# Zeros before x, two negations and one column copy on VectorE, and a new order of column pairs in a fused 2-D FFT gate kernel

## The chip, the cores and the metric

The kernel runs on one core of a Trainium2 chip. The metric is device time in microseconds (us) of one launch. Three runs of the kernel before gave 127.18 us as median (126.7 to 127.91). A separate, profiled execution of it took 127.11 us; its span from the first to the last recorded instruction is 125.3 us. All places in time below (such as "at 53.6") count from the start of that span.

## The reference

x has 2048 rows (S) of 1024 values (D), bf16. For each of two weight sets A and B the reference takes the real 2-D FFT of x, multiplies it elementwise by complex weights of 2048 x 513, and transforms back. A gate, one number per row of x, mixes the two results:

```
g = sigmoid((x * gate_w).sum(-1, keepdims=True))
X = rfft2(x);   a = irfft2(X * (A_w_r + 1j*A_w_i));   b = irfft2(X * (B_w_r + 1j*B_w_i))
return g * a + (1 - g) * b
```

## The kernel before, in words

All transforms are matrix products on TensorE (PE) with constant matrices. The program is written as one list of operations per engine (`P.add`); each engine works its own list strictly in order, and waits are derived from the keys that an operation reads (`r`), writes (`w`) or adds to (`a`). So an operation that waits holds up everything behind it on its engine, DMA issues included: those are on the lists of SP, POOL and ACT.

**Stage 1** (L337 to L400). x arrives in four blocks c = 0 to 3, each of four row groups. VectorE (DVE) folds each block (`fold`, L345: sums h = 0 and differences h = 1 of mirrored columns) into one of two halves of XF. PE multiplies the folds with a constant M and its negative (L380), 32 matmuls of 256 columns per block, into four PSUM places u = 2h + j of two banks each. The four places of a block are copied out to FT, 128x1024 at a time, by ScalarE (ACT, L389) or by DVE (L387); DVE has one of the four in each block. The next block writes the same place only after this copy. The negatives of M are made by ACT (`negate`, L359), 512 columns per block.

**Stages 2 to 4** (L425 to L491, `step`). 16 column pairs i are handled in turn: 8 pairs p of the transform along S, for two halves hf of the columns. `fold3` (DVE, L431) makes further sums. `stage2(i)` multiplies FT with F2 (PE, L443 and L452) into a pair of banks b0 and ACT copies it out (L458). `stage4(i)` multiplies this with CK (PE, L473), ACT copies it out as X(i) (L477), and `swap(i)` exchanges the partition halves of X(i) by two DMAs into XS(i). `product(i, 0)` multiplies X(i), and `product(i, 1)` XS(i), with the weights of pair p on DVE (L490, 128x2048). Step i runs stage4(i) and swap(i), then stage2(i + 2). The order of the products is written out in ORDER. Before, stage2 uses banks 0 and 1 for i = 0, 2 to 8, 10, 12 and 14, and banks 6 and 7 for 9, 11, 13 and 15. Column 512 is kept apart: `save512` (POOL, L527 and L528) saves it and puts column 256 in its place, and `star_products` (POOL, L532) multiplies it.

The gate's spectrum (`gate_spectrum`, L502) is collected in bank 6 on PE, two of its parts behind each of the steps 0 to 5, and copied out (L652) at the end.

The weights arrive by 44 DMAs on SP's list in six parts W0 to W5 (rows t = 0, 1 to 3, 4 to 7, 8 to 11, 12 and 13, 14 and 15); pair p needs rows 2p and 2p + 1.

**Stage 5** (`group`, L594, copies L602 and L604): 32 groups of 16 matmuls. Groups 0 to 15 need all products of hf = 0, groups 16 to 31 all of hf = 1. Between them lie the gate's sums (`zsum`, L541), the first column (`col0`, L568) and the star column (L507). **Stages 6 and 7** (L725, L750 and after) make the output rows; DVE makes their right-hand sides, `rbgen` (L581), during stage 5.

Of the kernel before, what the change touches and what calls it, by code (L numbers as in the profile page):

```python
# [234 lines left out]
def bass_gated_mix__spectral_gfnet__spectral_gfnet__prompt_kernel(nc, A_x, A_w_r, A_w_i, B_x, B_w_r, B_w_i, gate_w, out):  # L235
# [63 lines left out]
    XPARTS = {0: ((0, 1), (1, 1), (2, 2)), 1: ((0, 2), (2, 2)), 2: ((0, 4),), 3: ((0, 2), (2, 2))}  # L299
    XALL = [("x", c, q0) for c in range(4) for q0, n in XPARTS[c]]  # L300
    P.add("pool", lambda e: e.memset(DUM[:], 0.0), w=["DUM"])
    P.add("pool", lambda e: e.memset(sl(CL, GRo, [(1, 256)]), 0.0), w=["GRz"])
    def mload(eng, c0, n):
# [9 lines left out]
    load("F2", F2, 0, 1536, cst["F2"].ap(), w=["F2"])  # L313
    dma("sp", "GR", sl(CL, GRo, [(1, 128)], np_=8), AP(gate_w.tensor, gate_w.offset, [[128, 8], [1, 128]]), r=["GRz"], a=["GR"])
    load("CK", CK, 0, 1056, cst["CK"].ap(), w=["CK", "GW2"])
# [21 lines left out]
    def fold(c, q0, n, h):  # L337
        t, o = xloc(c)
        o += q0 * 1024
        fo = (c % 2) * 4096 + q0 * 1024  # L340
        for s in range(2):
            g = 1 - 2 * s
            i0 = sl(t, o + 511 * s, [(1024, n), (256 * g, 2), (g, 128)])
            i1 = sl(t, o + (512 if s else 1023), [(1024, n), (-256 * g, 2), (-g, 128)])
            P.add("dve", lambda e, s=s, i0=i0, i1=i1: e.tensor_tensor(  # L345
                out=sl(XF, fo + h * 512 + s * 256, [(1024, n), (384 - 512 * s, 2), (1, 128)]), in0=i0, in1=i1, op=ALU.subtract if h else ALU.add),
                r=[("x", c, q0)], w=[("xf", c % 2, q, h, s) for q in range(q0, q0 + n)])

# [8 lines left out]

    def negate(c):
        P.add("act", lambda e: e.activation(sl(MM, 2048 + c * 512, [(1, 512)]), sl(MM, c * 512, [(1, 512)]), ACT.Copy, scale=-1.0),  # L359
              r=[("M", c)], w=[("NM", c)])  # L360

    cnt = 0

    def stage1(c):
# [4 lines left out]
        for q0, n in parts:  # L369
            for h in range(2):  # L370
                for j in range(2):
# [13 lines left out]
                    dst = sl(FT, h * 8192 + j * 2048 + 4 * c, [(4096, 2), (16, 128), (1, 4)])  # L385
                    if (h == 1 and j == 0 and c < 3) or (c == 3 and h == 0 and j == 1):
                        P.add("dve", lambda e, s=src, d=dst: e.tensor_copy(d, s), r=[bank(2 * u), bank(2 * u + 1)], a=[("F1", h, j)])  # L387
                    else:
                        P.add("act", lambda e, s=src, d=dst: e.activation(d, s, ACT.Copy), r=[bank(2 * u), bank(2 * u + 1)], a=[("F1", h, j)])  # L389
                if h == 0 and c + 2 < 4 and q0 + n == 4:  # L390
                    negate(c + 2)

# [3 lines left out]
    folds(1)  # L396
    for c in range(4):
        stage1(c)
        if c + 2 < 4:
            folds(c + 2)  # L400

# [23 lines left out]
    def fold3(i, css=(0, 1)):  # L425

        n = len(css)
        for s, op in enumerate((ALU.add, ALU.subtract)):
            src = [sl(FT, 12288 * css[0] + j * 2048 + i * 256, [(12288, n), (1, 256)]) for j in range(2)]
            dst = sl(FT, 12288 * css[0] + s * 2048 + (i - 2) * 256, [(12288, n), (1, 256)]) if i > 1 else sl((EO, VD)[i], 512 * css[0] + 256 * s, [(512, n), (1, 256)])  # L430
            P.add("dve", lambda e, dst=dst, src=src, op=op: e.tensor_tensor(out=dst, in0=src[0], in1=src[1], op=op),  # L431
                  r=[("F1", cs, j) for cs in css for j in range(2)] + [("FR", i)], w=[("E", i, cs, s) for cs in css] + [("FR", i - 2)], a=["VD"] * (i == 1))

    def stage2(i, css=(0, 1), ab=(0, 1)):
        hf, p = divmod(i, 8)
        b0 = 4 if i == 1 else 6 if i in (9, 11, 13, 15) else 0
        if 0 in ab:
# [22 lines left out]

    n4 = 0

    def stage4(i):
        nonlocal n4
        b0 = 2 + 2 * (n4 % 2 if i < STEP5 else 0)
        n4 += 1
        parts = [(1, 0, 1), (0, 1, 1)] if i % 8 == 0 else [(0, 0, 2)]
        for pm in range(2):
# [11 lines left out]
    def swap(i):  # L480
        eng = ("pool", "sp")[i // 8]
# [4 lines left out]
    def product(i, sw):  # L486
        hf, p = divmod(i, 8)
        xt, xo, xk = (MM, XSo(i), ("XS", i % NX)) if sw else (XF, Xo(i), ("X", i % NX))
        at = lambda k: sl(WT[k], 4 * p * RWS[k] + 128 * hf, [(32 * RWS[k], 2), (RWS[k] // 2, 8), (1, 128)])
        P.add("dve", lambda e: e.tensor_tensor(out=at(sw), in0=sl(xt, xo, [(0, 2), (128, 8), (1, 128)]), in1=at(1), op=ALU.mult),  # L490
              r=[xk] + [("c256", p // 4)] * hf + [("W", need[t]) for t in (2 * p, 2 * p + 1)], a=[("prod", sw, hf)])  # L491

# [12 lines left out]
    def star_column(b):  # L505
# [5 lines left out]
        for ri in range(2):  # L511
            dma("pool", "xst", sl(XST, 32, [(1, 32)], p0=1 - ri, np_=64, pstep=2), sl(XST, 0, [(1, 32)], p0=ri, np_=64, pstep=2),
                r=["XST"], **({"a": ["XSS"]} if ri else {"w": ["XSS"]}))
# [8 lines left out]

    def save512(k):

        at = lambda l: sl(WA, 16 * k * RW + l, [(32 * RW, 2), (RW, 16)])
        wk = WK[3 * k:3 * k + 3]
        P.add("pool", lambda e: e.tensor_copy(sl(W5, 16 * k, [(32, 2), (1, 16)]), at(512)), r=wk, w=[("W5", k)])  # L527
        P.add("pool", lambda e: e.tensor_copy(at(512), at(256)), r=wk + [("W5", k)], w=[("c256", k)])  # L528

    def star_products():  # L530
        for sw in range(2):
            P.add("pool", lambda e, sw=sw: e.tensor_tensor(out=sl(PST, sw * 64, [(32, 2), (1, 32)]), in0=sl(XST, 32 * sw, [(0, 2), (1, 32)]),  # L532
                                                           in1=sl(W5, 0, [(32, 2), (1, 32)]), op=ALU.mult),
                  r=["XST", "XSS", ("W5", 0), ("W5", 1)], a=["PST"])
# [21 lines left out]
    def col0(u, sw):  # L556
# [10 lines left out]
        for n, (o, tc, rh) in enumerate(seq):  # L567
            P.add("pe", lambda e, o=o, tc=tc, rh=rh, n=n: e.matmul(o, sl(CL, tc, [(1, 128)]), rh, start=(n == 0), stop=(n == 7)),  # L568
                  r=["CL", "PST", ("prod", sw, 0)], w=[bank(bk)])
        P.add("act", lambda e: e.activation(sl(t, 0, [(RWS[sw], 64)]), ps(o0, [(1, 64)]), ACT.Copy),  # L570
# [16 lines left out]
    def group(u, g, eng):  # L587
        hf = g // 16
        for q in range(8):
            l0 = 8 * g + q  # L590
            o = ps(u * 1024 + q * 128, [(1, 128)])
            for ab in range(2):
                deps = [("prod", ab, hf), "CL"] + [("col0", ab)] * (g == 0)
                P.add("pe", lambda e, o=o, l0=l0, ab=ab: e.matmul(  # L594
# [21 lines left out]
    for i in range(2, 8):  # L616
        fold3(i)
# [5 lines left out]
    def step(i):  # L623
        nonlocal last2
        stage4(i)
        swap(i)
        if i == 5:
            save512(0)

        if i + 2 < 16:  # L630
            last2 = stage2(i + 2)
        if i == 8:
            save512(1)
# [3 lines left out]
    ORDER = (((0, 0),), ((1, 0),), ((2, 0),), ((3, 0), (0, 1)), ((1, 1),), ((2, 1), (4, 0)), ((3, 1), (5, 0)), ((4, 1),),  # L637
             ((5, 1),), ((6, 0), (6, 1)), ((8, 0),), ((7, 0), (7, 1), (8, 1)), ((9, 0), (9, 1)), ((10, 0), (10, 1), (11, 0), (11, 1)))

    def products(i):  # L640
        for n, sw in ORDER[i]:
            product(n, sw)

    last2 = None
    for i in range(8):
        step(i)
        for _ in range(2):
            if gt < 16:
                gate_spectrum(gt)
                gt += 1  # L650
        if i == 5:
            P.add("act", lambda e: e.activation(GSB[:], ps(6 * 512, [(1, 32)]), ACT.Copy), r=[bank(6)], w=["GSB"])  # L652
        products(i)
    for i in range(8, STEP5):
        step(i)
        products(i)
        if i == 12:
            row_sums()
# [15 lines left out]
    groups(1)  # L674
    star_column(2 * spare())
    star_products()
    groups(1)
    for i in (12, 14):
        for sw in range(2):
            product(i, sw)  # L680
    step(15)
    slots.insert(3, 1)
    groups(8)
    for i in (13, 15):
        for sw in range(2):
            product(i, sw)
    zsum(spare(), 0)
    groups(2)
    u = spare()
    for sw in range(2):  # L690
        col0(u, sw)
    gate_mask(0)
    for k, name in enumerate(("DI", "DJ")):
        dma("sp", name, sl(FT, DIo + k * 4096, [(2048, 2), (1, 1024)]).bitcast(u16), cst[name].ap().rearrange("p (a b) -> p a b", a=2), w=[name], after=[last2])
    groups(len(todo))
    for n, g in enumerate(range(16, 32)):
# [189 lines left out]
```

## Time and profile before

| what | value |
|---|---|
| median of three runs | 127.18 us |
| profiled execution: own time, span | 127.11 us, 125.3 us |
| PE, DVE, ACT, POOL busy | 112.7, 101.5, 98.8, 44.0 us |
| DMA engines busy, 5 to 44 us | all the time, 345 to 424 GB/s |
| stage 1, first to last matmul | 5.28 to 22.5 us |
| steps, up to the first matmul of stage 5 | to 53.6 us |
| stage 5 to the first matmul of stage 6 | 53.6 to 89.2 us |
| stages 6 and 7 and the last stores | 89.2 to 125.3 us |

Busy time is an average over stages with different limits. The chain of waits, which is followed back from the last instruction, tells which engine was last at each point; the timeline of an engine tells when its instructions start, and in brackets how long it idled before and for what. Copies overlap a little with the next instruction of their engine, so the distance from start to start is shorter than the duration, and it is the distance that sums up.

### The profile page before, as it was taken

How to read it: one execution, taken by the hardware profiler on the slowest of the kernel's cores; microseconds unless marked ns; L12 is line 12 of the kernel's file. 1: busy time of each engine (PE TensorE's matmuls, PEld its weight loads, DVE VectorE, ACT ScalarE, POOL GpSimd, SP SyncE). 2: the span in 40 equal slices, each digit the busy share in tenths (PEclk: the TensorE clock that was granted, in tenths of full speed). 3: DMA queues.
4: the chain of work that ended last, by engine and by line, in shares of the span. 5: the costliest groups of instructions: out<-in, count | busy, mean ns of one | idle time of the engine just before them, and what ended most of it. 6: DMA issues, size and time to landing. Idle time of an engine off the chain costs nothing.

```text
span 125.3 us, 3710 instructions
## 1 busy us (share of the span) xinstructions
PE 112.7 (90%) x1570; PEld 95.6 (76%) x1570; DVE 101.5 (81%) x157; ACT 98.8 (79%) x118; POOL 44.0 (35%) x53
## 2 busy tenths in 40 slices
PE   0399999799999999999999999999799999999950
PEld 0278787595757765579999999999799989898630
DVE  0578999799693999999999969999844778877890
ACT  4228986699999999999999997779589869687610
POOL 1000010006466803103071000000008999999980
PEclk9999999999999999999999999999999999999995
DMA  3999999999999997349993000000000242426265
GB/s 77 316 414 424 404 345 357 347 350 354 361 367 361 358 379 293 140 136 309 332 404 132 5 0 5 0 5 0 0 5 0 84 159 97 167 103 233 91 239 182
DMA packets 17505, 26.12 MB, mean 208 GB/s; under 512 B 2000, under 2 KB 10960, under 8 KB 17360
## 3 DMA queue, kind: packets, MB, share of 16 engines
q1 hardware_dynamic: 16224, 23.25, 53.0%
q0 software_dynamic: 832, 2.11, 4.6%
q10 hardware_dynamic: 432, 0.52, 1.4%
q8 instruction: 12, 0.20, 0.6%
q14 instruction: 5, 0.04, 0.1%
HBM read 17.48 MB, written 4.19 MB: 173 GB/s over the span
## 4 chain that ended last, share of the span: by engine, by line
PE 71%; DVE 8%; ACT 7%; DMA 5%; issue 3%; SPq 2%; DVEq 0%
PE PS L594 25%; PE PS L750 13%; PE PS L725 12%; PE PS L473 9%; DMA WB<-in_A_x_dram 5%; DVE XF L345 5%; PE PS L443 4%; ACT XF L458 3%; PE PS L502 2%; PE PS L452 2%; ACT XF L477 2%; DVE FT L387 2%; SPq L290 2%; PE PS L380 2%; PE PS L541 1%
## 5 line engine op out<-in xcount | busy, mean ns | idle before, releaser
L802 POOL TENSOR_TENSOR WA<-WA 128x512 bf16<-128x512 f32 x22 | 27.3, 1291 | 28.4 <-DVE WA L797 28.2
L594 PE MATMUL PS<-CL,WB 128*128 128x128 bf16 x256 | 32.0, 226 | 0.0
L594 PE MATMUL PS<-CL,WA 128*128 128x128 bf16 x256 | 31.8, 223 | 0.0
L594 PEld LDWEIGHTS PS<-CL,WB 128*128 128x128 bf16 x256 | 31.3, 145 | 0.6 <-issue 0.4
L594 PEld LDWEIGHTS PS<-CL,WA 128*128 128x128 bf16 x256 | 31.4, 145 | 0.1
L604 ACT ACTIVATE WB<-PS 128x1024 bf16<-128x1024 f32 (+1 forms) x29 | 27.9, 1039 | 2.3 <-PE PS L594 2.2
L380 PE MATMUL PS<-MM,XF 128*128 128x256 bf16 x128 | 16.9, 299 | 5.8 <-DVE XF L345 5.3
L490 DVE TENSOR_TENSOR WA<-MM,WA 128x2048 bf16<-128x2048 bf16 x16 | 19.5, 1233 | 2.3 <-DMA MM<-XF 2.3
L735 ACT ACTIVATE WA<-PS 128x1024 bf16<-128x1024 f32 (+1 forms) x16 | 15.8, 997 | 6.7 <-PE PS L725 6.7
L490 DVE TENSOR_TENSOR WB<-XF,WA 128x2048 bf16<-128x2048 bf16 x16 | 19.6, 1233 | 1.0 <-ACT XF L477 1.0
L380 PEld LDWEIGHTS PS<-MM,XF 128*128 128x128 bf16 x128 | 13.4, 107 | 9.0 <-DVE XF L345 5.2
L797 DVE TENSOR_TENSOR WA<-PS,WA 128x512 f32<-128x512 f32 x22 | 14.2, 686 | 6.7 <-ACT WA L757 4.2
L750 PE MATMUL PS<-FT,WA 128*128 128x256 bf16 (+1 forms) x132 | 19.3, 292 | 0.0
L477 ACT ACTIVATE XF<-PS 128x1024 bf16<-128x1024 f32 x16 | 17.4, 1085 | 0.9 <-PE PS L473 0.6
L458 ACT ACTIVATE XF<-PS 128x1024 bf16<-128x1024 f32 x16 | 16.9, 1062 | 0.6 <-PE PS L452 0.6
L473 PE MATMUL PS<-XF,CK 128*128 128x512 bf16 (+1 forms) x72 | 16.5, 356 | 0.6
L750 PEld LDWEIGHTS PS<-FT,WA 128*128 128x128 bf16 x132 | 12.3, 98 | 3.2
L290 POOL DMA_DIRECT2D MM<-XF x16 | 8.9, 555 | 16.3 <-PE PS L473 11.5
L389 ACT ACTIVATE FT<-PS 128x1024 bf16<-128x1024 f32 x12 | 11.6, 1035 | 3.4 <-PE PS L380 3.4
L443 PEld LDWEIGHTS PS<-F,FT 128*128 128x128 bf16 x128 | 7.9, 98 | 4.4 <-ACT XF L458 2.8
L345 DVE TENSOR_TENSOR XF<-WB 128x512 bf16<-128x512 bf16 (+1 forms) x20 | 6.0, 366 | 6.1 <-DMA WB<-in_A_x_dram 6.1
L443 PE MATMUL PS<-F,FT 128*128 128x128 bf16 x128 | 10.0, 220 | 0.1
(74 smaller groups left out, 137.5 us busy)
## 6 DMA issues: line engine op xcount, KB each, us to landing
out_dram<-WA SPq DMA_DIRECT2D x14, 256.0 KB, 2.1
MM<-XF POOLq DMA_DIRECT2D x16, 128.0 KB, 5.4
MM<-XF SPq DMA_DIRECT2D x16, 128.0 KB, 3.5
FT<-c_U SPq DMA_DIRECT2D x1, 2048.0 KB, 10.6
WB<-in_A_x_dram SPq DMA_DIRECT2D x3, 512.0 KB, 6.1
WA<-in_A_w_r_dram SPq DMA_DIRECT2D x4, 256.5 KB, 6.3
WA<-in_A_w_i_dram SPq DMA_DIRECT2D x4, 256.5 KB, 6.5
WA<-in_B_w_r_dram SPq DMA_DIRECT2D x4, 256.5 KB, 6.3
```

Source lines behind the costliest of these rows:

```text
L380: P.add("pe", lambda e, o=o, lh=lh, rh=rh, s=s: e.matmul(o, lh, rh, start=(s == 0), stop=(s == 1)), r=[("xf", c % 2, q, h, s ^ j), ("M", c ...
L443: P.add("pe", lambda e, o=o, cs=cs, j=j, t=t, rh=rh: e.matmul(o, fblock(1 + cs, j, t), rh, start=(j == 0), stop=(j == 1)), r=[("F1", cs, j ...
L458: P.add("act", lambda e: e.activation(dst, src, ACT.Copy), **kw)
L473: P.add("pe", lambda e, o=o, kind=kind, pm=pm, m=m, rh=rh: e.matmul(o, sl(CK, fbo(kind, pm, m), [(1, 128)]), rh, start=(m == 0), stop=(m = ...
L477: P.add("act", lambda e: e.activation(dst, ps(b0 * 512, [(256, 2), (512, 2), (1, 256)]), ACT.Copy), r=[bank(b0), bank(b0 + 1)], w=[("X", i ...
L490: P.add("dve", lambda e: e.tensor_tensor(out=at(sw), in0=sl(xt, xo, [(0, 2), (128, 8), (1, 128)]), in1=at(1), op=ALU.mult), r=[xk] + [("c2 ...
L594: P.add("pe", lambda e, o=o, l0=l0, ab=ab: e.matmul(o, sl(WT[ab], l0, [(RWS[ab] // 2, 128)]), sl(CL, KIo[ab], [(1, 128)]), start=(ab == 0) ...
L604: P.add("act", lambda e, s=src, d=dst: e.activation(d, s, ACT.Copy), r=b, a=["Z"])
L725: P.add("pe", lambda e, o=o, lh=lh, rh=rh, cp=cp: e.matmul(o, lh, rh, start=(cp == 0), stop=(cp == 1)), r=["Z", ("RB", r)], w=[bank(b0 + b ...
L735: P.add("act", lambda e, s=src, d=dst: e.activation(d, s, ACT.Copy), **kw)
L750: P.add("pe", lambda e: e.matmul(ps(col, [(1, n * 256)]), lh, rh, start=(k == 0), stop=(k == last)), r=[("Y", r), "DI"] + ["DJ"] * (full o ...
L802: P.add("pool", lambda e, s=s, op=op: e.tensor_tensor(out=ods(s, 0, 2), in0=pv[:, :, 0, :], in1=pv[:, :, 1, :], op=op), r=[("PQ", pk, 0), ...
```

## The change

Seven edits go together:

- 18 matmuls over zeros (256 columns each, into bank 7) stand at the head of PE's list. They read the part of CL that POOL sets to zero; POOL now does this before the other memset. The load of gate_w into that part now waits for these matmuls.
- `negate` for blocks 2 and 3 becomes one 128x1024 instruction on DVE.
- DVE copies out three places of stage 1, (c, h, j) = (1,0,1), (2,1,1) and (3,0,1), instead of four; block 0 is copied out by ACT alone. The folds of blocks 2 and 3 stand together ahead of blocks 2 and 3 on DVE, and the first four folds of block 2 are 128x512.
- The pairs go in the order SEQ: pair 0 of the second columns (hf = 1) is i = 3, so that pair 7 of the first columns is i = 8 instead of 7. The last products of both halves (i = 8 and 15) are cut in two halves of the columns, and groups wait only for their own half. All of stage2 from i = 2 on uses banks 0 and 1, but for 13 and 15.
- The gate's spectrum has one part per step (two in step 0) and ends in step 10. `fold3(6)` and `fold3(7)` move behind steps 0 and 1, and the keys of fold3 are per j.
- `save512` and `star_products` are on DVE, in steps 1 and 9 and late in the products. The star column's two small DMAs move from POOL to SP.
- The load U5 moves from step 13 to step 15.

```
+    for _ in range(18):
+        P.add("pe", lambda e: e.matmul(ps(7 * 512, [(1, 256)]), sl(CL, GRo, [(1, 128)]), sl(CL, GRo, [(1, 256)]), start=True, stop=True),
+              r=["GRz"], w=[bank(7)])
...
-    dma("sp", "GR", ..., r=["GRz"], a=["GR"])
+    dma("sp", "GR", ..., w=["GRz"], a=["GR"])
...
+        if eng == "dve":
+            P.add("dve", lambda e: e.tensor_scalar(out=dst, in0=src, scalar1=-1.0, scalar2=None, op0=ALU.mult), **kw)
...
-                    if (h == 1 and j == 0 and c < 3) or (c == 3 and h == 0 and j == 1):
+                    if (c, h, j) in ((1, 0, 1), (2, 1, 1), (3, 0, 1)):
...
-    for c in range(4):
-        stage1(c)
-        if c + 2 < 4:
-            folds(c + 2)
+    negate(2, 2, "dve")
+    stage1(0)
+    stage1(1)
+    fold(2, 0, 2, 0)
+    fold(2, 2, 2, 0)
+    fold(2, 0, 4, 1)
+    folds(3)
+    stage1(2)
+    stage1(3)
...
+    SEQ = [(0, 0), (0, 1), (0, 2), (1, 0)] + [(0, p) for p in range(3, 8)] + [(1, p) for p in range(1, 8)]
...
-        b0 = 4 if i == 1 else 6 if i in (9, 11, 13, 15) else 0
+        b0 = 4 if i == 1 else 6 if i in (13, 15) else 0
...
-            dma("pool", "xst", ...
+            dma("sp", "xst", ...
...
+        s0, n = ((0, 4), (4, 28))[k]
+        wk = WK[:2] if k == 0 else WK[1:]
+        if part == 0:
+            P.add("dve", lambda e: e.tensor_copy(sl(W5, s0, [(32, 2), (1, n)]), at(512)), r=wk, w=[("W5", k)])
+        else:
+            P.add("dve", lambda e: e.tensor_copy(at(512), at(256)), r=wk + [("W5", k)], w=[("c256", k)])
...
-                deps = [("prod", ab, hf), "CL"] + [("col0", ab)] * (g == 0)
+                deps = [("prod", ab, hf, g // 8 % 2), "CL"] + [("col0", ab)] * (g == 0)
...
-        if i == 13:
+        if i == 15:
             dma("sp", "U5", ...
...
+    ORDER = (((0, 0),), ((1, 0),), ((2, 0),), ((3, 0),), ((0, 1), (4, 0)), ((1, 1), (2, 1), (5, 0)), ((3, 1), (6, 0)), ((4, 1), (7, 0)),
+             ((5, 1), (8, 0, 0, 1)), ((6, 1), (7, 1)), ((8, 1, 0, 1), (8, 0, 1, 1), (8, 1, 1, 1), (9, 0)), ((9, 1), (10, 0)), ((10, 1), (11, 0)), ((11, 1), (12, 0)))
...
+    for a in ((13, 1), (14, 1), (15, 0, 0, 1), (15, 1, 0, 1), (15, 0, 1, 1), (15, 1, 1, 1)):
+        product(*a)
...
```

More of the change, by code (lines that the diff above doesn't have):

```diff
@@ L356, in folds, with negate @@
             fold(c, q0, n, h)
-    def negate(c):
-        P.add("act", lambda e: e.activation(sl(MM, 2048 + c * 512, [(1, 512)]), sl(MM, c * 512, [(1, 512)]), ACT.Copy, scale=-1.0),
-              r=[("M", c)], w=[("NM", c)])
+    def negate(c, n=1, eng="act"):
+        dst, src = sl(MM, 2048 + c * 512, [(1, n * 512)]), sl(MM, c * 512, [(1, n * 512)])
+        kw = dict(r=[("M", k) for k in range(c, c + n)], w=[("NM", k) for k in range(c, c + n)])
+        if eng == "dve":
+            P.add("dve", lambda e: e.tensor_scalar(out=dst, in0=src, scalar1=-1.0, scalar2=None, op0=ALU.mult), **kw)
+        else:
+            P.add("act", lambda e: e.activation(dst, src, ACT.Copy, scale=-1.0), **kw)
     cnt = 0
@@ L484, in swap, with product @@
                 r=[("X", i % NX)], **({"a": [("XS", i % NX)]} if ri else {"w": [("XS", i % NX)]}), after=last1)
-    def product(i, sw):
-        hf, p = divmod(i, 8)
+    def product(i, sw, h0=0, n=2):
+        hf, p = SEQ[i]
         xt, xo, xk = (MM, XSo(i), ("XS", i % NX)) if sw else (XF, Xo(i), ("X", i % NX))
-        at = lambda k: sl(WT[k], 4 * p * RWS[k] + 128 * hf, [(32 * RWS[k], 2), (RWS[k] // 2, 8), (1, 128)])
-        P.add("dve", lambda e: e.tensor_tensor(out=at(sw), in0=sl(xt, xo, [(0, 2), (128, 8), (1, 128)]), in1=at(1), op=ALU.mult),
-              r=[xk] + [("c256", p // 4)] * hf + [("W", need[t]) for t in (2 * p, 2 * p + 1)], a=[("prod", sw, hf)])
+        at = lambda k: sl(WT[k], 4 * p * RWS[k] + 128 * hf + 64 * h0, [(32 * RWS[k], 2), (RWS[k] // 2, 8), (1, 64 * n)])
+        P.add("dve", lambda e: e.tensor_tensor(out=at(sw), in0=sl(xt, xo + 64 * h0, [(0, 2), (128, 8), (1, 64 * n)]), in1=at(1), op=ALU.mult),
+              r=[xk] + [("c256", p > 0)] * hf + [("W", need[t]) for t in (2 * p, 2 * p + 1)], a=[("prod", sw, hf, h) for h in range(h0, h0 + n)])
     def gate_weights(b):
@@ L521, in row_sums, with save512 @@
         P.add("dve", lambda e: e.tensor_copy(AB[:], AT[:]), r=["AT"], w=["AB"])
[L523 to L528, printed above, removed]
+    def save512(k, part):
+        s0, n = ((0, 4), (4, 28))[k]
+        at = lambda l: sl(WA, s0 * RW + l, [(32 * RW, 2), (RW, n)])
+        wk = WK[:2] if k == 0 else WK[1:]
+        if part == 0:
+            P.add("dve", lambda e: e.tensor_copy(sl(W5, s0, [(32, 2), (1, n)]), at(512)), r=wk, w=[("W5", k)])
+        else:
+            P.add("dve", lambda e: e.tensor_copy(at(512), at(256)), r=wk + [("W5", k)], w=[("c256", k)])
     def star_products():
         for sw in range(2):
-            P.add("pool", lambda e, sw=sw: e.tensor_tensor(out=sl(PST, sw * 64, [(32, 2), (1, 32)]), in0=sl(XST, 32 * sw, [(0, 2), (1, 32)]),
-                                                           in1=sl(W5, 0, [(32, 2), (1, 32)]), op=ALU.mult),
+            P.add("dve", lambda e, sw=sw: e.tensor_tensor(out=sl(PST, sw * 64, [(32, 2), (1, 32)]), in0=sl(XST, 32 * sw, [(0, 2), (1, 32)]),
+                                                          in1=sl(W5, 0, [(32, 2), (1, 32)]), op=ALU.mult),
                   r=["XST", "XSS", ("W5", 0), ("W5", 1)], a=["PST"])
@@ L615, in bass_gated_mix__spectral_gfnet__spectral_gfnet__prompt_kernel @@
                 gate_weights(7)
-    for i in range(2, 8):
+    for i in range(2, 6):
         fold3(i)
@@ L650, in bass_gated_mix__spectral_gfnet__spectral_gfnet__prompt_kernel @@
                 gt += 1
-        if i == 5:
+        if i == 10:
             P.add("act", lambda e: e.activation(GSB[:], ps(6 * 512, [(1, 32)]), ACT.Copy), r=[bank(6)], w=["GSB"])
+        if i in (1, 9):
+            save512(i // 8, 0)
         products(i)
-    for i in range(8, STEP5):
-        step(i)
-        products(i)
+        if i in (1, 9):
+            save512(i // 8, 1)
+        if i < 2:
+            fold3(6 + i)
         if i == 12:
@@ L675, in bass_gated_mix__spectral_gfnet__spectral_gfnet__prompt_kernel @@
     star_column(2 * spare())
+    groups(1)
+    product(12, 1)
+    product(13, 0)
     star_products()
[L677 to L680, printed above, removed]
+    product(14, 0)
     step(15)
@@ L683, in bass_gated_mix__spectral_gfnet__spectral_gfnet__prompt_kernel @@
     groups(8)
-    for i in (13, 15):
-        for sw in range(2):
-            product(i, sw)
+    for a in ((13, 1), (14, 1), (15, 0, 0, 1), (15, 1, 0, 1), (15, 0, 1, 1), (15, 1, 1, 1)):
+        product(*a)
     zsum(spare(), 0)
-    groups(2)
+    gate_mask(0)
+    for k, name in enumerate(("DI", "DJ")):
+        dma("sp", name, sl(FT, DIo + k * 4096, [(2048, 2), (1, 1024)]).bitcast(u16), cst[name].ap().rearrange("p (a b) -> p a b", a=2), w=[name], after=[last2])
+    groups(3)
     u = spare()
@@ L691, in bass_gated_mix__spectral_gfnet__spectral_gfnet__prompt_kernel @@
         col0(u, sw)
[L692 to L695, printed above, removed]
+    groups(3)
     for n, g in enumerate(range(16, 32)):
```

39 lines of the change are left out of this document (14 added, 25 removed).

## The prediction

> **What bounds the kernel now.** I read the chain of waits first, then the timelines of the engines that it names. The chain, columns start and length in us:
>
> ```profile
> 16.72 2.85 DVE XF L345 x8
> 19.58 1.14 DVE FT L387
> 20.72 0.05 issue
> 20.77 1.92 PE PS L380 x16
> ...
> 53.63 1.13 PE PS L594 x16
> ...
> 56.74 7.78 PE PS L594 x128
> ```
>
> DVE sets the time up to 20.7; from 53.6 PE has no gap worth naming before 88.5. So everything turns on when PE gets into stage 5, and on whether something holds it there. DVE's timeline in stage 1:
>
> ```profile
> 12.04 1.22 DVE L387 CAST FT<-PS 128x1024 bf16<-128x1024 f32 x1
> 13.17 2.50 DVE L345 TENSOR_TENSOR XF<-WA 128x1024 bf16<-128x1024 bf16 x4
> 15.59 1.22 DVE L387 CAST FT<-PS 128x1024 bf16<-128x1024 f32 x1
> 16.72 2.85 DVE L345 TENSOR_TENSOR XF<-WA 128x512 bf16<-128x512 bf16 x8
> 19.50 2.34 DVE L387 CAST FT<-PS 128x1024 bf16<-128x1024 f32 x2
> ```
>
> No brackets: DVE idles nowhere from 10.02 (x arrives) on. Start to start, a copy costs 1.14, a 128x1024 fold 0.60, a 128x512 fold 0.34. TensorE's clock in stage 1, from the matmuls of L380 in three equal stretches (two shown; after the stretch come its length, PE's busy time and its matmuls):
>
> ```profile
> 7.60:10.00 2.40, 2.40 (x13) 1.71 (x12) 1.00 1.06 431
> 10.20:12.60 2.40, 2.40 (x24) 2.15 (x23) 1.00 0.98 408
> ```
>
> Matmuls start 213 ns apart until 10.1 and 109 ns apart after it, though the clock column says 1.00 in both. But PE was not the bound there: DVE was.
>
> The steps, ACT's timeline:
>
> ```profile
> 32.23 1.02 ACT L458 ACTIVATE XF<-PS 128x1024 bf16<-128x1024 f32 x1
> ...
> 34.24 1.02 ACT L458 ACTIVATE XF<-PS 128x1024 bf16<-128x1024 f32 x1
> ```
> ```profile
> 51.38 1.17 ACT L458 ACTIVATE XF<-PS 128x1024 bf16<-128x1024 f32 x1
> ...
> 53.18 1.19 ACT L458 ACTIVATE XF<-PS 128x1024 bf16<-128x1024 f32 x1
> ```
> ```profile
> 33.30 0.45 PEld L443 LDWEIGHTS PS<-F,FT 128*128 128x128 bf16 x8 [0.51 <-ACT XF L458]
> ```
>
> Late steps take 1.81, two copies of 0.904: ACT bounds. While stage2 has one bank pair, its weight load waits for the copy (1.02 + 0.05), and the next copy starts 0.94 after: a loop of 2.01 per step, however idle ACT is. Last, what the products wait for:
>
> ```profile
> 48.89 0.49 POOL L527 COPY W<-WA 128x32 bf16<-128x32 bf16 x1 [5.04 <-DMA WA<-in_B_w_i_dram]
> ```
> ```profile
> 70.64 1.22 DVE L490 TENSOR_TENSOR WA<-MM,WA 128x2048 bf16<-128x2048 bf16 x1
> ```
>
> The last weights (W5) are there at 48.9. The last product ends at 71.86, and group 16 starts at 71.9: PE and DVE arrive together.
>
> **Stage 1.** DVE's copy of block 0 goes. In its place comes the negation; a TENSOR_SCALAR of 128x1024 (L550) runs 0.48 and holds the next instruction for 0.40 to 0.51. No row shows it without its per-partition scalar: bounds 0.34 (a 128x512 fold) and 0.60 (a 128x1024 fold), taken 0.40. So 12.04 + 0.40 = 12.44; copy (1,0,1) to 13.58; four folds to 14.92; two to 16.12; eight (2.78) to 18.90; copy (2,1,1) to 20.04. PE: x lets block 1's first half start its second rows at 10.8, so with a fast clock it is through at 12.2, ahead of 12.44. Block 2 has its first half folded at 15.0, with 4 of its matmuls done. From there 60 matmuls remain for PE, 60 x 0.109 = 6.55, to 21.6; the folds (16.2 and 18.95) come before PE needs them (16.4 and 19.8), the banks too: ACT's 10 copies of 0.92 are at most one behind, and (2,1,1) ends 0.7 before its place is needed at 20.7. Before, the last matmul started its 109 ns at 22.4 (20.77 + 16 x 0.109 = 22.52 for the end of issue). Gain **0.92**, and what follows, ACT's last copy, moves with PE.
>
> The zeros run from 1.1 (memset 0.31 after 0.74): 18 x 0.213 = 3.84, to 4.95, under the wait for x (5.28), so they cost nothing; each one more would cost 0.21. SP reaches gate_w's load at 6.50, after them; if they were late, all weights behind it on SP would be. Their use is small: they take the slow matmuls out of block 0, which only (1,0,1) would feel. [...]
>
> **Steps.** Let a be the start of the copy L458 of i = 2: 28.08 before, 27.16 after. Before, the steps to the copy of i = 8 took 12.44 (2.01 and 2.14 in turn: 16 gate matmuls, 0.38 on PE, and L652, 0.30 on ACT), the seven to i = 15 12.66. After, PE has one gate part less in each (-0.19), so the loop of 2.01 binds, and, as 9 and 11 now use banks 0 and 1 too, up to i = 12: 10 x 2.01 = 20.1. Then bank 6, free after L652 (+0.20): copies of 13, 14, 15 at a + 22.2, 24.0, 25.8; stage4(13)'s copy runs from a + 24.93 to a + 25.95 and frees the banks of the first group: a + 26.0 = 53.16, against 53.60 before. So the steps **lose 0.48** of the 0.92. The first 6 steps gain 0.4, the next 4 lose 4 x 0.2, the rest is L652 and the banks. Pair (1,0) at i = 3 takes 8 narrow matmuls for 4 (1.04 against 0.89), inside ACT's slack in the loop.
>
> **From 53 on.** PE's work is the same and has no gap, so 0.44 is kept if DVE has the products. (8,0,0,1) needs W5, so DVE stands still from some 46 to 48.9; the bytes ahead of W5 are the same. Behind it before group 16: 14 full products (1.144: 16.0), six halves (as 128x1024, 0.60: 3.6), row sums 1.53, two copies of save512 and two star products. These small ones have no row on DVE; 0.09 (L521, start to start) to 0.49 (POOL's longer L527) each, taken 0.13, nearest L521: 0.5. Together 21.7: 48.9 + 21.7 = 70.6, 0.8 before PE's 71.44. (8,1,0,1) is done at 52.6, before group 1; (8,0,1,1) at 53.3, and X(14) writes its buffer at 53.9. Then DVE's second halves end at 71.8, as before, and its idle of 1.4 up to 88 takes up the 0.44.
>
> Nothing for: U5 (SP issues it behind swap 15, about 58.5; 10.6 to land makes 69.1, rbgen starts at 72.9); DI and DJ behind it (needed at 91); the star DMAs (swap 15 behind them waits until 57.7 anyway); fold3 (two later pairs, DVE idle there). save512 off POOL lets swap 6 go earlier; nobody waits then.
>
> **Sum.** 127.11 - 0.92 + 0.48 = 126.67. The profiled run is 0.07 under the median, so about **126.7**. Bounds of the negation (-0.06, +0.2; faster than 0.25 it would wait for PE) and of the small ones (four at 0.49: +1.4, of which 0.8 is slack) give 126.5 to 127.3.
>
> **Rivals.**
> - A: zeros do not raise the clock. For it: only real data is in the trace. Then block 1's first half is done at 13.1, as before, copy (1,0,1) waits 0.66, and 126.67 + 0.66 = 127.3. 0.08. [...]
> - B: the bank loop opens, and steps go at ACT's 1.81. Then (8,1,0,1) stops PE at 52.65 instead: gain 0.95, 126.2. Against it: all six waits of L443 name L458. 0.11.
> - C: B, and W5 lands 0.6 sooner, as POOL's swaps move out of its way: groups start at 52.05, group 16 at 70.3; gain 1.55, 125.6. For it: the DMA engines are full until 48. 0.16.
> - D, slower: the weights become the bound. DVE stands in order at (8,0,0,1), with all later products, swaps 12 to 15 (which need buffers that these free) and group 1 behind it; slack 0.8, so from a landing at 49.7 it holds group 16, from 50.2 the kernel is slower than before. With the longest landing in the page (10.7 after issue) on the last issue at 41.55, W5 comes at 52.25, group 16 at 73.95: 2.05 late, 129.2. For it: DVE reaches W5 with one product fewer behind it than before and loses 3 us there. 0.12.
> - Forecast: 0.53.
>
> Range: all but D, 125.5 to 127.7. Faster by over 1% (about what a measurement can tell here; below 125.9) is C: 0.16; slower (above 128.45) is D: 0.12; within, 0.72.
>
> **What would show it.** Right: DVE copies (1,0,1) at 12.4; last L380 near 21.6; L458 every 2.01 from i = 2 to 12; DVE idle for W5 up to 48.9; first L594 near 53.2. Wrong: L380 still 213 ns after 8; L458 at 1.81 before i = 12; a PE gap at group 16; W5 far from 48.9.

## The result, and the profile after

The changed kernel takes 126.15 us as median of 12 runs (125.62 to 126.41); the kernel before, run beside it on the same chip, 127.07. The ratio is 0.992, with a 95% interval of 0.990 to 0.995: 0.9 us faster by the medians, forecast 0.44. (Some runs, of the kernel before above all, were disturbed and took 129 to 135; they are left out of all ratios and medians here, and of the one experiment whose profile fell into such a run only the stretch behind the last matmul is read.)

The profiled execution took 126.23 us, its span 124.3. The chain that ended last, columns start and length:

```profile
13.54 0.98 DVE XF L348 x3
15.02 6.62 PE PS L387 x59
21.72 1.03 ACT FT L396
...
53.17 1.13 PE PS L606 x16
54.37 1.03 PE PS L606 x16
...
88.62 1.96 PE PS L735 x32
```

From 15.0 on PE, not DVE, carries stage 1 (its matmuls are L387 now; L606 is stage 5, L735 stage 6). DVE's timeline there:

```profile
12.07 0.42 DVE L365 TENSOR_SCALAR MM<-MM 128x1024 bf16<-128x1024 bf16 x1
12.41 1.22 DVE L394 CAST FT<-PS 128x1024 bf16<-128x1024 f32 x1
13.54 5.30 DVE L348 TENSOR_TENSOR XF<-WA 128x512 bf16<-128x512 bf16 x14
18.77 2.38 DVE L394 CAST FT<-PS 128x1024 bf16<-128x1024 f32 x2
```

The negation, start to start, is 0.34, and no bracket stands behind the copy at 12.41: PE had its input ready. The zeros on PE's timeline, and then the matmuls L387 from 7.2 to 9.0 (after the stretch its length, and PE's busy time with its matmuls):

```profile
1.10 4.02 PE L304 MATMUL PS<-CL 128*128 128x256 bf16 x18 [1.10 <-POOL DUM L302]
```
```profile
7.20:9.00 1.80, 1.80 (x18) 1.43 (x16) 1.00 1.02 402
```

The kernel before has 10 matmuls in the same stretch. Single records show the pitch, the distance from one matmul's start to the next, falling from 213 to 109 ns at some 7.1; before, at some 10.1. The steps, from ACT's timeline (L470 is the former L458):

```profile
27.03 1.02 ACT L470 ACTIVATE XF<-PS 128x1024 bf16<-128x1024 f32 x1
...
45.11 1.02 ACT L470 ACTIVATE XF<-PS 128x1024 bf16<-128x1024 f32 x1
...
47.12 1.02 ACT L470 ACTIVATE XF<-PS 128x1024 bf16<-128x1024 f32 x1
...
52.85 1.06 ACT L470 ACTIVATE XF<-PS 128x1024 bf16<-128x1024 f32 x1
```

The first line is i = 2, the third i = 12, the last i = 15. Ten steps from i = 2 to i = 12 take 20.09, the loop of 2.01 each. And DVE at the last weights:

```profile
48.89 0.70 DVE L499 TENSOR_TENSOR WB<-XF,WA 128x1024 bf16<-128x1024 bf16 x1 [1.20 <-DMA WA<-in_B_w_i_dram]
49.51 0.20 DVE L538 COPY W<-WA 128x56 bf16<-128x56 bf16 x1
```

W5 is there at 48.89, to the hundredth as before (by chance, as later profiles show). Where the time went, term by term (us, profile against profile):

| stretch | forecast | before | after | measured |
|---|---|---|---|---|
| start of the last stage-1 matmul | -0.92 | 22.41 | 21.36 | -1.05 |
| from there to the first matmul of stage 5 | +0.48 | 31.19 | 31.77 | +0.58 |
| from there to the first of stage 6 | 0 | 35.57 | 35.49 | -0.08 |
| from there to the end of the span | 0 | 36.15 | 35.65 | -0.50 |
| execution outside the span | 0 | 1.79 | 1.96 | +0.17 |
| sum | -0.44 | | | -0.88 |

The steps of the forecast hold within 0.13. The term that it doesn't have is the fourth: within it, the stretch from the last matmul's end to the last packet of the stores took 3.75 before and 3.28 after.

### The profile page after: what moved, and what is told of

Same layout as the page of the kernel before. It is cut to its first block, busy times and chain, and to the rows that moved or that the text cites. A ratio compares the mean times of both kernels' runs of the same rounds, so it can differ in the third digit from the quotient of the medians.

```text
span 124.3 us, 3754 instructions
## 1 busy us (share of the span) xinstructions
PE 116.1 (93%) x1588; PEld 96.6 (78%) x1588; DVE 100.9 (81%) x169; ACT 100.0 (80%) x117; POOL 38.6 (31%) x45
## 4 chain that ended last, share of the span: by engine, by line
PE 73%; ACT 11%; DMA 6%; DVE 4%; issue 2%; SPq 2%; DVEq 0%
PE PS L606 25%; PE PS L760 13%; PE PS L735 12%; ACT XF L470 8%; PE PS L387 7%; PE PS L455 6%; DMA WB<-in_A_x_dram 6%; PE PS L481 4%; PE PS L464 3%; DVE XF L348 2%; SPq L290 2%; DVE WA L771 1%; PE PS L553 1%; ACT FT L396 1%; ACT XF L485 1%
## 5 line engine op out<-in xcount | busy, mean ns | idle before, releaser
L606 PE MATMUL PS<-CL,WB 128*128 128x128 bf16 x256 | 31.9, 226 | 0.0
L606 PE MATMUL PS<-CL,WA 128*128 128x128 bf16 x256 | 31.7, 223 | 0.0
L606 PEld LDWEIGHTS PS<-CL,WB 128*128 128x128 bf16 x256 | 31.3, 145 | 0.6 <-DVE WA L499 0.4
L606 PEld LDWEIGHTS PS<-CL,WA 128*128 128x128 bf16 x256 | 31.4, 145 | 0.1
L499 DVE TENSOR_TENSOR WB<-XF,WA 128x2048 bf16<-128x2048 bf16 (+1 forms) x18 | 20.0, 1110 | 3.6 <-DMA WA<-in_B_w_i_dram 2.1
L499 DVE TENSOR_TENSOR WA<-MM,WA 128x2048 bf16<-128x2048 bf16 (+1 forms) x18 | 19.8, 1111 | 0.6 <-DMA MM<-XF 0.6
L470 ACT ACTIVATE XF<-PS 128x1024 bf16<-128x1024 f32 x16 | 16.3, 1025 | 0.7 <-PE PS L464 0.6
L485 ACT ACTIVATE XF<-PS 128x1024 bf16<-128x1024 f32 x16 | 16.5, 1034 | 0.3 <-PE PS L481 0.2
L387 PE MATMUL PS<-MM,XF 128*128 128x256 bf16 x128 | 16.2, 284 | 0.5 <-DVE XF L348 0.3
L387 PEld LDWEIGHTS PS<-MM,XF 128*128 128x128 bf16 x128 | 12.6, 101 | 4.2 <-DVE XF L348 2.2
L396 ACT ACTIVATE FT<-PS 128x1024 bf16<-128x1024 f32 x13 | 12.4, 1028 | 2.2 <-PE PS L387 2.2
```

The costliest lines, as they stand in the source:

```text
L387: P.add("pe", lambda e, o=o, lh=lh, rh=rh, s=s: e.matmul(o, lh, rh, start=(s == 0), stop=(s == 1)), r=[("xf", c % 2, q, h, s ^ j), ("M", c ...
L470: P.add("act", lambda e: e.activation(dst, src, ACT.Copy), **kw)
L485: P.add("act", lambda e: e.activation(dst, ps(b0 * 512, [(256, 2), (512, 2), (1, 256)]), ACT.Copy), r=[bank(b0), bank(b0 + 1)], w=[("X", i ...
L606: P.add("pe", lambda e, o=o, l0=l0, ab=ab: e.matmul(o, sl(WT[ab], l0, [(RWS[ab] // 2, 128)]), sl(CL, KIo[ab], [(1, 128)]), start=(ab == 0) ...
```

## The experiments

### Stage 1 alone, and all but stage 1

The kernel before with the edits of stage 1 (zeros, negation, order, copies) and nothing else; and the changed kernel with the old stage 1.

```
 b_stage1: before.py, and
+    for _ in range(18): ... matmul over zeros
+    negate(2, 2, "dve")
+    stage1(0); stage1(1); folds of 2 and 3; stage1(2); stage1(3)
+    if (c, h, j) in ((1, 0, 1), (2, 1, 1), (3, 0, 1)):
 a_old_st1: after.py, and these lines as in before.py
```

> The kernel before with the stage 1 of the change alone (zeros, negation on DVE, three copies, order of the folds); pairs, banks, gate, products and column 512 as before. Theory 1: stage 1 ends 1.05 us earlier and the old steps take it along without the 0.5 that the new banks cost, PE would enter stage 5 near 52.6 and group 16 near 70.9; DVE gains too, as its old wait for the swap of pair 2 (2.06 us up to 39.96) gets shorter and W5 lands at 48.9: 0.9 to 1.0 us faster than before. Theory 2: DVE has no slack at group 16 in the old order, it stays bound by DMA landings, and most of the gain is lost there: 0 to 0.4 us faster than before, with a gap of PE ahead of group 16.

> The changed kernel with stage 1 as before: no zeros, both negations of blocks 2 and 3 on ScalarE, the old evictions and the old order. It has the later parts alone: the pair (1,0) at the fourth step, the banks, column 512 and the star products on VectorE, the swaps and halves. Theory 1 (the later parts by themselves lose what the steps lost, 0.58, less the 0.08 of group 16): last stage-1 matmul near 22.4, L470 of i = 2 near 28.1, first matmul of stage 5 near 54.1, stage 6 near 89.7, and if the end behind the last matmul is the 3.3 of the changed kernel, 127.2 in the median; with 3.7, 127.6. Theory 2 (the later parts bring a gain of their own, which stage 1 hides): under 126.9.

Stage 1 alone: 126.28 us, ratio 0.992 (0.987 to 0.996). All but stage 1: 127.06 us, ratio 1.0015 (0.9998 to 1.003). So the whole gain is stage 1's, and the later parts, all together, bring nothing that can be measured: what they lose in the steps they win back at the end, as the profiles below show. The length of stage 1, from DVE's first fold of the last of x to PE's last matmul, settles its term:

| kernel | first fold | last matmul | length |
|---|---|---|---|
| before | 10.02 | 22.41 | 12.39 |
| all but stage 1 | 9.88 | 22.20 | 12.32 |
| stage 1 alone | 10.03 | 21.34 | 11.31 |
| after | 10.05 | 21.36 | 11.31 |

The five other experiments that keep the whole changed stage 1 have 11.31 too; x lands there between 9.69 and 10.06 and moves all of it along. Behind it, all but stage 1 came to stage 5 at 53.97, 31.77 after its last stage-1 matmul, exactly as the changed kernel: the lost half microsecond of the steps is theirs. Its stretch behind the last matmul is 3.30, stage 1 alone has 3.40: both less than the 3.75 of before. That left the cause of the fourth term open, see the last group.

Stage 1 alone did what its first theory says, as far as its profile goes: stage 5 starts at 52.53, group 16 at 70.78, and stage 6 at 88.02, 0.60 before that of the changed kernel. Its profiled run, 125.57, is the faster by 0.66. But its runs spread from 125.27 to 127.10, those of the changed kernel from 125.62 to 126.41, and the medians differ by 0.13 the other way. Its last product ends at 70.76, right at group 16, where the changed kernel has 0.7 to spare (its products of the first halves end at 70.63, group 16 starts at 71.36). That this missing slack makes the spread is likely, but not shown.

### The zeros

```
 a_no_zeros: after.py without            b_zeros: before.py with (and the memsets and gate_w's load as in after.py)
-    for _ in range(18):
-        P.add("pe", lambda e: e.matmul(ps(7 * 512, [(1, 256)]), ... r=["GRz"], w=[bank(7)])
```

> The changed kernel without the 18 matmuls over zeros (gate_w's load then waits for nothing of PE), all else as changed. My theory (rival A of the prediction, turned round): the clock then rises near 10 us as before, block 1's first half is through PE at about 13.0 instead of 12.3, DVE's copy (1,0,1) starts near 13.1 instead of 12.4, and all later stages slide by this: 0.6 to 0.7 us slower than the changed kernel, about 126.8. Rival: PE's clock in stage 1 is hidden anyway, and the time is that of the changed kernel, 126.15.

> The kernel before with the 18 matmuls over zeros alone. Theory 1 (the clock rises near 7 instead of 10, but VectorE bounds stage 1, so nothing follows): last stage-1 matmul 22.3 to 22.4, stage 6 within 0.1 of 89.17, 127.1 to 127.4, ratio 0.998 to 1.002. Theory 2 (the zeros alone carry the gain): last stage-1 matmul before 22.0 and a ratio under 0.996. On the stretch from the last matmul to the last packet of the stores: 3.7 if it belongs to the kernel before's later parts, 3.3 to 3.4 if it goes with the zeros (the run of the stage-1 edits alone had 3.40).

Without zeros the changed kernel takes 126.44 us (ratio 0.994, 0.991 to 0.997); with them the kernel before takes 126.91 (1.0007, 0.997 to 1.004). Without zeros, the same stretch (its matmuls are L384), and then DVE's timeline:

```profile
7.20:9.00 1.80, 1.80 (x11) 1.20 (x9) 1.00 1.00 388
```
```profile
12.17 0.42 DVE L362 TENSOR_SCALAR MM<-MM 128x1024 bf16<-128x1024 bf16 x1
12.69 1.23 DVE L391 CAST FT<-PS 128x1024 bf16<-128x1024 f32 x1
```

PE is slow up to some 9.7 (11 matmuls in that stretch for 18), and DVE's copy starts 0.52 behind the negation instead of 0.34. Stage 1 takes 11.50, so in this profile the zeros are worth 0.19, not the 0.66 of rival A: that figure came from PE's place in the kernel before, and in this run PE was through with that half of block 1 0.4 sooner (its pitch fell 0.4 sooner, too). From the first zero matmul at 1.1 to the fall of the pitch are 2.8 to 6.0 us in the eight traces with zeros. In the kernel before the zeros are worth nothing: with them its pitch had fallen by 5.41 (the first matmuls of stage 1 are 109 ns apart), stage 1 still took 12.40, since DVE bounds it (it idles nowhere from 9.75 to its last copy). Its profile (127.79 us) shows instead a wait that can make times of the kernel before spread. The waits between 64 and 73, columns total, times and longest in us:

```profile
DVE WA L493 <- DMA MM<-XF: 0.8, 1, 0.8
```

and between 64 and 73 in the trace of the kernel before:

```profile
DVE WA L490 <- DMA MM<-XF: 0.2, 1, 0.2
```

The product of the swapped pair 14 waits for its swap, which SP issues behind the 2 MB of U5. As that kernel has no slack at group 16, the 0.8 went on to PE, which waited 0.9 there, and stage 6 came at 90.00 instead of within 0.1 of 89.17.

### The steps: banks and gate parts as before

```
 a_banks: after.py with
-        b0 = 4 if i == 1 else 6 if i in (13, 15) else 0
+        b0 = 4 if i == 1 else 6 if i in (9, 11, 13, 15) else 0
-        for _ in range(2 if i == 0 else 1):
+        for _ in range(2):
-        if i == 10:
+        if i == 5:
```

> The changed kernel with the old banks of stage2 (6 and 7 for i = 9, 11, 13, 15) and the old pace of the gate's spectrum (two parts per step, copied out in step 5). My theory says that the new banks cost 0.5 us: L458's successors at 1.81 from i = 9 on instead of 2.01, first matmul of stage 5 no longer held by banks but by product (8,1,0,1) at 52.73: 0.4 us faster than the changed kernel, about 125.75. Rival: the changed kernel is bound by DVE behind the last weights or by PE elsewhere, and nothing is gained (126.15).

125.72 us in four runs, ratio 0.9875 (0.981 to 0.994), an interval that takes in most of the changed kernel's; profile against profile 0.23 less. The copies of i = 8 to 15 are 1.8 apart again and the first matmul of stage 5 starts at 52.56 for 53.13. Not all of it stays, as the chain shows:

```profile
43.26 5.66 DMA WA<-in_B_w_i_dram
...
49.84 2.29 DVE WA L499 x2
52.13 0.20 DVE WA L540
52.33 0.54 DVE WA L499
52.87 0.05 issue
52.91 1.13 PE PS L606 x15
```

PE's second matmul waits to 52.91: group 1 now hangs on W5 and DVE's queue behind it. Stage 6 starts 0.24 before that of the changed kernel. So the chosen banks, with the gate parts that go with them, do cost 0.6 at the start of stage 5, and 0.35 of it is covered by the weights.

### What the weights and the halves carry

```
 a_late_w5: after.py with the 384 KB load of CL ahead of W5 instead of behind
 a_whole:   after.py with
-    (8, 0, 0, 1) ... (8, 1, 0, 1), (8, 0, 1, 1), (8, 1, 1, 1) ... (15, 0, 0, 1), ... (15, 1, 1, 1)
+    (8, 0) ... (8, 1) ... (15, 0), (15, 1)
```

> The changed kernel with the 384 KB load of CL ahead of the last weights W5 on SP's list instead of behind them: W5 lands about 1.1 us later (384 KB at 357 GB/s), near 50.0. Rival D of the prediction puts the slack at 0.8 at group 16, and 0.4 at group 1 (product (8,1,0,1) ends at 52.73, group 1 starts at 53.13): the kernel gets 0.6 to 0.8 us slower, first at group 1. If the weights are hidden, it is the same (126.15); if the kernel is bound by them now, the whole 1.1 is lost.

> The changed kernel with products 8 and 15 in one piece each, so that groups wait for all of them. By my sum of DVE's work behind W5 (48.9): product (8,1) ends at 53.7, so group 1 starts 0.55 later than 53.13, and the last product ends at 71.8, about when PE arrives at group 16. 0.5 to 0.6 us slower than the changed kernel, about 126.7. Rival: the halves only matter when the banks are not what holds group 1; then it is the same, 126.15.

With the load ahead: 126.51 us, ratio 0.9955 (0.992 to 0.999), its interval overlapping that of the changed kernel; the profiled runs are the same (126.21 and 126.23). W5 in this run, and in the one without zeros:

```profile
49.25 0.70 DVE L501 TENSOR_TENSOR WB<-XF,WA 128x1024 bf16<-128x1024 bf16 x1 [2.72 <-DMA WA<-in_B_w_i_dram]
```
```profile
48.32 0.70 DVE L496 TENSOR_TENSOR WB<-XF,WA 128x1024 bf16<-128x1024 bf16 x1 [1.68 <-DMA WA<-in_B_w_i_dram]
```

W5 came 0.36 later than in the changed kernel, not 1.1. Even that can't be put down to the edit: in the undisturbed profiles in which W5 keeps its place on SP's list it landed anywhere from 47.84 (zeros alone) over 48.32 (no zeros) and 48.89 (before, and after) to 49.36 (all but stage 1). What the run does show is the slack: with W5 at 49.25 the second matmul of stage 5 started at 53.14, right behind the product's end at 53.09. How the kernel does with weights later than that wasn't reached.

Whole products: 127.05 us, ratio 0.997 (0.994 to 1.000). PE at the start of stage 5:

```profile
52.93 0.25 PE L606 MATMUL PS<-CL,WB 128*128 128x128 bf16 x1
54.00 0.27 PE L606 MATMUL PS<-CL,WA 128*128 128x128 bf16 x1 [0.82 <-DVE WA L499]
```

PE stands 0.82 for the second half of the uncut (8,1), which ends at 53.95. Stage 6 starts at 89.45, 0.83 later than in the changed kernel: what is lost at group 1 is not won back. So in the changed kernel the halves are worth 0.8 to 0.9; without them it would hardly have been faster than the one before. What they mend came with the change, though: stage 1 alone, with whole products and the old order of pairs, has no such wait at the start of stage 5.

### A version that takes both

Old banks, the load of the row-sum constants behind all weights, and another order of the products around W5.

```
 a_best and a_best2: after.py with the edits of a_banks, and
-        if t0 == 8:
-            load("CV", ...)          (now behind the last weights)
-    ((5, 1), (8, 0, 0, 1)), ((6, 1), (7, 1)), ((8, 1, 0, 1), (8, 0, 1, 1), ...
 a_best:
+    ((5, 1), (8, 0, 0, 1)), ((8, 1, 0, 1), (6, 1)), ((8, 0, 1, 1), (7, 1), ...
 a_best2:
+    ((5, 1), (6, 1), (8, 0, 0, 1)), ((7, 1),), ((8, 1, 0, 1), (8, 0, 1, 1), ...
```

> The kernel of the run on banks (old banks of stage2, old pace of the gate) with two more edits: the 147 KB load CV goes behind all weights on SP's list, and product (8,1) of the first half is second behind W5, ahead of (6,1); then (8,0) of the second half, then (7,1). W5 should land up to 0.4 earlier, (8,1,0,1) ends 1.4 behind it, near 50.1, instead of 3.8, so group 1 is held by banks again, at 52.5, and X(14)'s buffer is free in time. 0.5 to 0.7 us faster than the changed kernel, 125.5; if DVE's last product stays where it is and PE waits at group 16, no faster than the run on banks (125.72).

The first was a miss: 127.16 us, ratio 0.998 (0.994 to 1.002). W5 landed 0.4 sooner, which lies within the spread above, but DVE could use none of it:

```profile
48.50 0.70 DVE L498 TENSOR_TENSOR WB<-XF,WA 128x1024 bf16<-128x1024 bf16 x1 [1.46 <-DMA WA<-in_B_w_i_dram]
49.12 0.20 DVE L537 COPY W<-WA 128x56 bf16<-128x56 bf16 x1
50.40 1.85 DVE L498 TENSOR_TENSOR WA<-MM,WA 128x1024 bf16<-128x1024 bf16 x2 [1.08 <-DMA MM<-XF]
```
```profile
54.18 0.27 PE L605 MATMUL PS<-CL,WA 128*128 128x128 bf16 x1 [1.74 <-DVE WA L498]
```

DVE waited 1.08 for the swap of pair 8, to which (8,1,0,1) had been moved up, and group 1 also reads (7,1), which had been moved behind (8,0,1,1): an error of the order, not of the banks.

> The changed kernel with the banks of the kernel before (bank 6 for 9, 11, 13, 15; two gate parts a step), the load of the row-sum constants behind all weights, and the product (6,1) put ahead of the wait for W5. Group 1 needs all products of the first eight pairs and their swapped ones, (6,1) and (7,1) too; the run before this one had put (7,1) behind (8,0,1,1), which held group 1 by 1.74. Now (6,1) lies in VectorE's idle time before W5, and behind W5, expected at 48.5, come (8,0,0,1), (7,1), (8,1,0,1), done by 51.3 if the swap of pair 8 is there at 50.4. Theory (group 1 is then held by banks and ScalarE's copies alone): first matmul of group 1 at 52.0 to 52.6 and no wait of its second, stage 6 0.5 to 0.6 before the changed kernel, 125.5 in the median, ratio to the kernel before 0.985. Rival (group 16 takes it back, as VectorE's later products end at 71.4 as before): stage 6 at most 0.25 earlier, 125.9.

125.59 us in five runs (125.38 to 125.62), ratio 0.990 (0.988 to 0.992); profile against profile 0.63 under the changed kernel. DVE around W5, and PE:

```profile
46.07 2.37 DVE L498 TENSOR_TENSOR WA<-MM,WA 128x2048 bf16<-128x2048 bf16 x2
48.58 0.70 DVE L498 TENSOR_TENSOR WB<-XF,WA 128x1024 bf16<-128x1024 bf16 x1
```
```profile
52.47 0.25 PE L605 MATMUL PS<-CL,WB 128*128 128x128 bf16 x1
52.55 0.22 PE L605 MATMUL PS<-CL,WA 128*128 128x128 bf16 x1
```

(6,1) fills what was idle time, no bracket is left, and (8,1,0,1) is done at 51.28, 1.2 before PE comes. Stage 6 starts at 87.98, 0.64 before that of the changed kernel, and the last product ends at 70.41, 0.3 before group 16: the rival, that group 16 takes it back, falls. This is the fastest of all kernels here by its median, though its interval touches that of the changed kernel. Up to stage 6 it only undoes what the later parts had lost: stage 1 alone is there at 88.02. What it has more is slack at group 16, 0.3 where stage 1 alone has 0.02, and its five runs lie within 0.24.

### Behind the last matmul

Two runs asked first whether the 0.47 there is chance, and whether U5 has to do with it: the kernel before once more, unchanged, and with `if i == 15:` for `if i == 13:` at the load U5.

> The kernel before itself, for a second profile of it. The change gained 0.9 us by the runs but 0.44 by my sum; between the two profiles 0.43 us lie behind the last matmul, in one late packet of the last store of before. Theory 1: that packet was chance, and what usually costs the kernel before the other 0.4 us is DVE without slack at group 16: in another profile the tail behind the last matmul is 3.3 as in all other profiles, and PE waits 0.2 to 0.6 us for a product ahead of group 16 (it waited 0.09). Theory 2: the late packet is a trait of before: the tail is 3.7 again. Ratio to before 1.000 within 0.3%.

> The kernel before with the 2 MB load U5 at step 15 instead of 13, nothing else. If the kernel before is held at group 16 by landings on a DVE without slack, the swaps of pairs 12 to 15 land sooner without U5 in their way, DVE's last product ends up to 0.25 us earlier than 71.86, and the time falls by 0 to 0.3 us, with a smaller spread. If PE alone sets the time there, it is the same (127.06).

Unchanged: ratio 1.001 (0.997 to 1.005), stretch 3.71. With U5 late: 126.95 us, ratio 0.998 (0.996 to 1.001), stretch 3.72. So it is no chance, and U5 is not the cause. (Late U5 does take the wait for the swaps away: the last product ended at 71.40 though x landed 0.38 later in that run. In time this can't be told from nothing.)

In the DMA view of the last 7 us, the kernel before has a transfer that the changed one lacks:

```profile
q1 hardware_dynamic: 798, 1.08, 42.8%
q10 hardware_dynamic: 288, 0.39, 15.8%
q14 instruction: 1, 0.01, 0.6%
...
out_dram<-WA SPq DMA_DIRECT2D x3, 256.0 KB, 2.9
...
out_dram<-WA SPq DMA_DIRECT2D x1, 128.0 KB, 2.4
```

It is the line of q14, a fetch of instructions, 8 KB in 0.66, and the stores of SP land 0.5 to 0.7 later than in the changed kernel (2.2 and 1.9). When that fetch starts, against the end of the last matmul, and how many records DVE has in the trace:

| kernel | DVE records | fetch starts | last packet |
|---|---|---|---|
| before; again; zeros alone; U5 late | 198 | -0.58; -0.55; -0.56; -0.58 | 3.75; 3.71; 3.66; 3.72 |
| stage 1 alone | 199 | -0.77 | 3.40 |
| whole products | 207 | -3.14 | 3.33 |
| all but stage 1 | 210 | -4.47 | 3.30 |
| after; five more with its DVE work | 211 | -5.57; -5.53 to -5.55 | 3.28; 3.29 to 3.30 |

The more records DVE has, the sooner the fetch starts: -0.55 to -0.58 with 198, -5.53 to -5.57 with 211. If DVE's instructions are the cause, it needs nothing but more of them:

```
 b_pad: before.py with
+    PAD = sb("PAD", 2, f32)
+    for _ in range(13):
+        P.add("dve", lambda e: e.memset(PAD[:], 0.0), w=["PAD"])
```

> The kernel before with 13 tiny memsets on VectorE at its start, in the 10 us in which it waits for x; nothing else. In the traces so far the stretch from the last matmul to the last packet of the stores is 3.66 to 3.75 where an 8 KB fetch of instructions starts 0.55 to 0.58 before the last matmul's end, 3.40 where it starts 0.77 before it, and 3.28 to 3.32 where it starts 3 or more before it; and the fetch comes the earlier, the more instructions VectorE has (198, 199, 207, 210, 211 records: 0.58, 0.77, 3.14, 4.47, 5.57 before the end). Theory (it is VectorE's code, and fetched that late it takes its place among the last stores): with 211 records the fetch moves to some 5.5 before the end, the stretch becomes 3.3, and the kernel gets 0.4 faster by instructions that do nothing: ratio near 0.997. Rival (the fetch is a bystander, and the stretch goes with other parts): the fetch moves, the stretch stays at 3.7, ratio 1.000; or the fetch doesn't move, and is another engine's.

The fetch moved to -5.37 and the stretch became 3.29, within a hundredth that of the changed kernel. (Another 8 KB fetch starts 4.2 before the last matmul's end in the kernel before and in this one, so that one is not the cause.) The same window of its DMA view has no q14 any more, and

```profile
q1 hardware_dynamic: 772, 1.02, 40.7%
q10 hardware_dynamic: 288, 0.39, 16.0%
...
out_dram<-WA SPq DMA_DIRECT2D x3, 256.0 KB, 2.3
...
out_dram<-WA SPq DMA_DIRECT2D x1, 128.0 KB, 1.9
```

126.70 us against 127.13, ratio 0.998 (0.995 to 1.001): by the medians the size expected, 0.4, though the interval still holds no change. In the profiles it is shown that the stretch depends on where this fetch falls. How 8 KB come to cost 0.47 is only argued: the DMA share is 0.95 from 121 to 124, with the stores, and the last five packets of 2 KB in the kernel before end 0.08 apart, up to 0.37 after all others, as if one DMA engine were behind by the 0.66 that the fetch took.

## Why the prediction was right, and where it was not

The verdict (within 1%) and the range held. The forecast of 126.7 was 0.5 too slow, and the faster rival C (125.6) would have missed by as much; but C's mechanism is not what happened. Stage 1 and the steps went as forecast; that the verdict held as well owes something to luck, since a term left out of the sum is as large as the whole forecast gain.

- **Stage 1**, forecast -0.92, measured -1.05. The bound passed from DVE to PE at 15.0 as put. The negation took 0.34, at the lower bound of its range, not 0.40, but PE still started at 15.02 for 15.0. The 0.13 is one matmul fewer from there on (59 in the chain, not 60: 0.11) and a sum rounded from 21.55 up to 21.6.
- **Steps**, forecast +0.48, measured +0.58. The loop of 2.01 up to i = 12 came out to the hundredth, the three copies behind it within 0.02 when counted from the measured copy of i = 2, 27.03 (49.22, 51.04, 52.85 for 49.23, 51.03, 52.83). ACT's last copy for group 1 ended as put, at 52.99 (27.03 + 26.0 = 53.03), but PE was at the matmuls of stage 4 until 53.13. Rival B, the open loop, falls; with the old banks the copies do run at 1.81.
- **Products.** "So 0.44 is kept if DVE has the products" held; (8,1,0,1) was done at 52.73 for 52.6, the products for group 16 at 70.63 for 70.6. But the slack was put in the wrong place: 0.8 at group 16, while the kernel hangs on group 1, where it was 0.4 (whole products cost 0.8 to 0.9, and W5 0.36 later used all of it). Rival D starts there, from a landing near 49.3, not from 49.7, and so within the spread of landings seen here.
- **W5** at 48.89: rival C's sooner landing did not come in this profile. The hit to the hundredth is luck, as other profiles with W5 in the same place have 47.8 to 49.4.
- **Zeros.** With them the pitch fell to 109 ns at 3.9 to 7.1, without them at 8.7 to 10.1, and rival A falls; but its price, 0.66, was 0.19 in the one profile that tests it. No run had shown by then that zeros bring the pitch down, so the "fast clock" that the sum gives block 1's first half (through at 12.2), and the 8 in "L380 still 213 ns after 8", rested on none. The sum did not hang on where the fall lies: the seven profiles with the whole changed stage 1 have 11.31 for it.
- **"Nothing for U5":** right for this kernel's time within what can be told; before, it cost DVE 0.2 to 0.8 in three traces, which an early group 16 would have felt.
- **The step that failed** is "From 53 on. PE's work is the same and has no gap, so 0.44 is kept": the forecast followed PE to its end and took what comes after it as fixed. The 0.50 behind stage 6 is nearly all of the miss (0.44), and it goes with the moment of the instruction fetch, 0.58 ahead of the last matmul's end before and 5.57 after, which 13 added DVE instructions alone moved to 5.37, not with the work of any edit. 0.17 of it is lost again outside the span, for no reason that the traces show.

## What to carry to other kernels

Add up a forecast to the last packet of the last store, not to the last matmul: a fetch of instructions in that stretch is a row of the profile, and here 13 instructions more on an idle engine moved it by 4.8 and the end by 0.46. When a bound is passed from one engine to the next, ask how much slack the next has at the first place that waits for it (group 1 here), not at the best known one. Put work that is ready into an engine's known idle time ahead of a late landing: one product moved there, with the old banks and one load moved back, brought 0.6 on the changed kernel. And run each part of a change alone: here stage 1 by itself came to stage 6 sooner than the whole.

## What was not expected of the hardware

- The instruction fetch: 8 KB on q14, 0.66 long. The stretch behind the last matmul took 3.75 where it starts 0.58 ahead of that matmul's end, 3.28 where it starts 5.57 ahead.
- The pitch falls behind matmuls over zeros as it does behind those over data. In the eight profiles with zeros, which start at 1.1, the pitch fell to 109 ns at 3.9 to 7.1; in the five undisturbed ones without, whose first matmul starts at 4.97 to 5.62, at 8.7 to 10.1. The clock column says 1.00 in both stretches; only the pitch tells.
- The landing of the same weights moves by 1.5 from profile to profile (47.84 to 49.36) with their place on the queue unchanged; the DMA engines are 90% busy or more from 30 to 48 in the kernel before. So one profile in which a landing comes 0.4 sooner or later doesn't show that an edit of the queue did it.
